# FAVOR+ attention feeding a GEGLU block on one core: attention of the next batch issued beside a token tile, elementwise work in large blocks, output projection as a separate pass

## The chip, the cores and the metric

The kernel runs on one core of a Trainium2 chip. The metric is device time in microseconds (us) of one execution. The engines are TensorE (PE; its weight loads are listed apart as PEld), VectorE (DVE), ScalarE (ACT), GpSimd (POOL) and SyncE (SP). In these kernels matmuls write their results to the memory called PSUM, and most other tiles lie in the one called SBUF. Most executions agree within half a per cent.

Every timed experiment ran beside the kernel before on the same chip. A ratio is the mean time of a kernel's fast runs over that of the kernel before in the same rounds, so it is not quite the quotient of the medians that are quoted beside it.

## The reference

There are 8 batches of 8 heads, 576 positions and 64 dimensions. The attention is linear: positive random features, no softmax matrix. Its output, as 4608 tokens of 512 numbers, goes through a GEGLU block of width 1536.

```python
q_s, k_s = q * scale, k * scale
def phi(x):                                   # 128 features a head
    h = x @ omega.T - sum(x * x) / 2
    return exp(h - max(h)) / sqrt(128)
kv  = phi(k_s).T @ v ;  z = phi(k_s).sum(over positions)
x   = (phi(q_s) @ kv) / (phi(q_s) @ z + 1e-6)  # to (4608, 512)
out = (gelu(x @ w_gate) * (x @ w_val)) @ w_out
```

The maximum is over the features of one position, so the `sum(x*x)` term cancels in it. For q any factor per position cancels in the quotient, so neither kernel takes a maximum for q. For k it must be taken, because the sum over positions weighs positions against each other. Both kernels append a column of ones to v, so that one matmul gives kv and z.

## The kernel before

The attention works head pair by head pair and in pieces of 128 positions. Each step hands a small tile from one engine to the next.

```python
for b in range(B):
    # 15 loads through GpSimd: k, v, q in pieces of 128 positions ...
    for jh in range(NH2):                      # pairs of heads
        for si, (s0, st) in enumerate(s_tiles):   # 5 pieces
            nc.tensor.transpose(kT_ps[:, :st], kslab[:, jh*P:(jh+1)*P], ident[:st, :st])
            nc.vector.tensor_copy(kT_sb[:, :st], kT_ps[:, :st])
            nc.tensor.matmul(proj_ps[:st], kT_sb[:, :st], omega2T)
            nc.vector.reduce_max(nmax[:st], proj_ps[:st]..., negate=True)
            for h2 in range(2):
                nc.scalar.activation(k_p_tiles[si]..., proj_ps..., func=Exp, bias=nmax[:st, h2, :])
        # kz_ps += k_p.T @ v_ext, copied to kz_sb, for the two heads ...
        _try_emit_il(b)        # one gate/value block of token tile 0, from batch 1 on
    for si, (s0, st) in enumerate(s_tiles):
        # transpose q, project, Exp, matmul with kz, divide, transpose x into xT_all ...
        _try_emit_il(b)
```

Only one of the nine token tiles (`N_IL = 1`) gets its gate and value matmuls under the attention. Their results are parked in SBUF and take their Gelu after the last Exp. The other eight tiles follow the attention:

```python
for ti in range(N_IL, N_TOK):
    for jf in range(N_DFF):                    # 12 blocks of 128 columns
        # 4 matmuls g_ps, 4 matmuls vv_ps (512 columns each)
        nc.scalar.activation(g_gelu, g_ps, func=Gelu)
        nc.vector.tensor_mul(gated, g_gelu, vv_ps)
        for q in range(NSUB):                  # output projection, 4 accumulators
            nc.tensor.matmul(out_ps_list[q], gated[:, q*P:(q+1)*P], w_out_sb[:, jf, :], ...)
```

The softmax here doesn't subtract the row's maximum and nothing guards it: scores larger than these inputs give would overflow.

Of the kernel before, what the change touches and what calls it, by code (L numbers as in the profile page):

```python
# [15 lines left out]
def kernel(  # L16
# [11 lines left out]
    nc = tc.nc  # L28
# [3 lines left out]
    assert D == D2  # L32
# [6 lines left out]
    scale = 1.0 / float(D) ** 0.25  # L39

    P = 128
    DFF_TILE = 128
    N_DFF = d_ff // DFF_TILE
    N_DM = d_model // P
    NH2 = H // 2

    singles = ctx.enter_context(tc.tile_pool(name="singles", bufs=1))

    ident = singles.tile([P, P], BF16)
    make_identity(nc, ident)  # L50


    with tc.tile_pool(name="tr_psum0", bufs=1, space=bass.MemoryType.PSUM) as tr_psum0:
        omega_f = singles.tile([M, D], F32)
        nc.sync.dma_start(out=omega_f, in_=omega)
        omega_bf = singles.tile([M, D], BF16)
        nc.scalar.mul(omega_bf, omega_f, scale)
        omegaT_ps0 = tr_psum0.tile([D, M], BF16)
        nc.tensor.transpose(omegaT_ps0, omega_bf, ident)
        omegaT = singles.tile([D, M], BF16)  # L60
        nc.vector.tensor_copy(omegaT, omegaT_ps0)
        omegaT2 = singles.tile([2 * D, M], BF16)
        nc.vector.tensor_copy(omegaT2[:D], omegaT_ps0)
        nc.vector.tensor_copy(omegaT2[D:], omegaT_ps0)
        omega2T = singles.tile([2 * D, 2 * M], BF16)
        nc.vector.memset(omega2T, 0.0)
        nc.vector.tensor_copy(omega2T[:D, :M], omegaT)
        nc.vector.tensor_copy(omega2T[D:, M:], omegaT)
# [3 lines left out]
    w_out_sb = singles.tile([P, N_DFF, d_model], BF16)  # L72

    xT_all = singles.tile([P, N_DM, n_tokens], BF16)

    wg = moe_w_gate.rearrange("(dmo dmi) f -> dmi dmo f", dmi=P)
    wv = moe_w_val.rearrange("(dmo dmi) f -> dmi dmo f", dmi=P)
    wo = moe_w_out.rearrange("(dfo dfi) m -> dfi dfo m", dfi=P)

    def _load_moe_weights():  # L80
        for j in range(N_DM):
            nc.gpsimd.dma_start(out=w_gate_sb[:, j, :], in_=wg[:, j, :])
            nc.gpsimd.dma_start(out=w_val_sb[:, j, :], in_=wv[:, j, :])
        for j in range(N_DFF):
            nc.gpsimd.dma_start(out=w_out_sb[:, j, :], in_=wo[:, j, :])

    DP1 = D + 1

    T_TOK = 512
    N_TOK = n_tokens // T_TOK  # L90
    NSUB = T_TOK // P
    assert n_tokens % T_TOK == 0

    N_IL = 1
    g_all_il = [singles.tile([DFF_TILE, N_DFF, T_TOK], F32, name=f"g_all_il{ti}")
                for ti in range(N_IL)]
    vv_all_il = [singles.tile([DFF_TILE, N_DFF, T_TOK], BF16, name=f"vv_all_il{ti}")
                 for ti in range(N_IL)]
    moe_psum = ctx.enter_context(tc.tile_pool(name="moe_psum", bufs=2, space=bass.MemoryType.PSUM))

    def _moe_gv_jf(ti, jf, ga, va):
        tok = ti * T_TOK
        xT = xT_all[:, :, tok:tok + T_TOK]
        g_ps = moe_psum.tile([DFF_TILE, T_TOK], F32, name="g_ps", tag="gv")
        for jm in range(N_DM):
            nc.tensor.matmul(  # L106
                g_ps, w_gate_sb[:, jm, jf * DFF_TILE:(jf + 1) * DFF_TILE],
                xT[:, jm, :], start=(jm == 0), stop=(jm == N_DM - 1))
        nc.vector.tensor_copy(ga[:, jf, :], g_ps)
        vv_ps = moe_psum.tile([DFF_TILE, T_TOK], F32, name="vv_ps", tag="gv")  # L110
        for jm in range(N_DM):
            nc.tensor.matmul(  # L112
                vv_ps, w_val_sb[:, jm, jf * DFF_TILE:(jf + 1) * DFF_TILE],
                xT[:, jm, :], start=(jm == 0), stop=(jm == N_DM - 1))
        nc.vector.tensor_copy(va[:, jf, :], vv_ps)

    def _il_gen():
        for ti in range(N_IL):
            for jf in range(N_DFF):
                yield ti, jf  # L120
    _il_iter = _il_gen()
    _il_next_b = [1]

    def _try_emit_il(b):
        if b < _il_next_b[0]:
            return
        unit = next(_il_iter, None)
        if unit is None:
            _il_next_b[0] = B + 1
            return  # L130
        ti, jf = unit
        _moe_gv_jf(ti, jf, g_all_il[ti], vv_all_il[ti])
        _il_next_b[0] = ti + 1


    phase1 = ExitStack()
    in_pool = phase1.enter_context(tc.tile_pool(name="in", bufs=2))
    tr_psum = phase1.enter_context(tc.tile_pool(name="tr_psum", bufs=1, space=bass.MemoryType.PSUM))
    work = phase1.enter_context(tc.tile_pool(name="work", bufs=3))
    proj_psum = phase1.enter_context(tc.tile_pool(name="proj_psum", bufs=2, space=bass.MemoryType.PSUM))  # L140
    nd_psum = phase1.enter_context(tc.tile_pool(name="nd_psum", bufs=1, space=bass.MemoryType.PSUM))
    kz_psum_pool = nd_psum
    kz_pool = phase1.enter_context(tc.tile_pool(name="kz", bufs=1))
    xpool = phase1.enter_context(tc.tile_pool(name="x", bufs=2))

    s_tiles = []
    s0 = 0
    while s0 < S:
        st = min(P, S - s0)
        s_tiles.append((s0, st))  # L150
        s0 += st

    k_v = k.rearrange("b h s d -> b s h d")
    q_v = q.rearrange("b h s d -> b s h d")
    v_v = v.rearrange("b h s d -> b s h d")

    NS = len(s_tiles)

    for b in range(B):
        k_in = in_pool.tile([P, NS, H, D], BF16, name="k_in")  # L160
        q_in = in_pool.tile([P, NS, H, D], BF16, name="q_in")
        v_ext = in_pool.tile([P, NS, H, DP1], BF16, name="v_ext")
        nc.vector.memset(v_ext[:, :, :, D:D + 1], 1.0)
        for si, (s0, st) in enumerate(s_tiles):
            nc.gpsimd.dma_start(out=k_in[:st, si], in_=k_v[b, s0:s0 + st, :, :])  # L165
        for si, (s0, st) in enumerate(s_tiles):
            nc.gpsimd.dma_start(out=v_ext[:st, si, :, :D], in_=v_v[b, s0:s0 + st, :, :])  # L167
        for si, (s0, st) in enumerate(s_tiles):
            nc.gpsimd.dma_start(out=q_in[:st, si], in_=q_v[b, s0:s0 + st, :, :])  # L169

        if b == 1:
            _load_moe_weights()

        kz_sb = kz_pool.tile([M, H, DP1], BF16, name="kz_sb")

        for jh in range(NH2):
            h0 = 2 * jh
            k_p_tiles = [work.tile([P, 2 * M], BF16, name=f"k_p{si}", tag=f"k_p{si}")
                         for si in range(NS)]
            for si, (s0, st) in enumerate(s_tiles):  # L180
                kslab = k_in[:st, si, :, :].rearrange("s h d -> s (h d)")
                kT_ps = tr_psum.tile([P, P], BF16, name="kT_ps", tag="trp")
                nc.tensor.transpose(kT_ps[:, :st], kslab[:, jh * P:(jh + 1) * P],  # L183
                                    ident[:st, :st])
                kT_sb = work.tile([P, P], BF16, name="kT_sb")
                nc.vector.tensor_copy(kT_sb[:, :st], kT_ps[:, :st])  # L186

                proj_ps = proj_psum.tile([P, 2 * M], F32, name="proj_ps", tag="prj")
                nc.tensor.matmul(proj_ps[:st], kT_sb[:, :st], omega2T)  # L189

                nmax = work.tile([P, 2, 1], F32, name="nmax")
                nc.vector.reduce_max(nmax[:st],  # L192
                                     proj_ps[:st].rearrange("s (h m) -> s h m", h=2),
                                     axis=mybir.AxisListType.X, negate=True)
                for h2 in range(2):
                    nc.scalar.activation(k_p_tiles[si][:st, h2 * M:(h2 + 1) * M],
                                         proj_ps[:st, h2 * M:(h2 + 1) * M],
                                         func=mybir.ActivationFunctionType.Exp,
                                         bias=nmax[:st, h2, :], scale=1.0)
            for h2 in range(2):  # L200
                h = h0 + h2
                kz_ps = kz_psum_pool.tile([M, DP1], F32, name="kz_ps", tag="nd0")
                for si, (s0, st) in enumerate(s_tiles):
                    nc.tensor.matmul(kz_ps, k_p_tiles[si][:st, h2 * M:(h2 + 1) * M],  # L204
                                     v_ext[:st, si, h, :],
                                     start=(si == 0), stop=(si == NS - 1))
                nc.vector.tensor_copy(kz_sb[:, h, :], kz_ps)  # L207
# [142 lines left out]
```

## Time and profile before

| | |
|---|---|
| time | 574.18 us, median of 3 (573.97 to 574.81) |
| profiled span | 570.9 us |
| first stage: attention, with one tile's gate/value | about 288 us |
| second stage: the other eight tiles | about 283 us |
| one token tile in the second stage | 32.9 us |
| 144 matmuls x 0.216 us, what such a tile streams | 31.1 us |

These rows of the profile page cut the span into 40 equal slices of 14.3 us. A digit is the busy share in tenths. PEclk is the clock that the throttle granted to TensorE.

```profile
PE   3688997767677686767489999999999999999994
DVE  4566876656556565565423242422324242332423
ACT  4563565656656565665822222222222222222220
PEclk9998988756655555565679999999999999999998
```

The two stages are plain to see. From slice 21 on TensorE is full at full clock. Before that no engine stays full, and from slice 7 the clock is at 0.5 to 0.7. The next table has one line per stretch: length, busy time (and instructions) of each engine, granted clock, DMA share, GB/s.

```profile
160.00:180.00 20.00, 15.89 (x124) 9.44 (x123) 12.20 (x45) 11.87 (x30) 12.58 (x15) 0.50 1.24 78
340.00:380.00 40.00, 40.00 (x176) 15.91 (x175) 12.90 (x19) 8.96 (x15) 0.00 (x0) 1.00 0.07 28
```

In the first of these stretches TensorE counts as busy for 79% of the time (72% over the whole first stage), yet the timeline shows mostly the latency of lone matmuls at half clock. The timeline shows one step of the chain (start, length, engine, line, operation, output and inputs, and in brackets how long the engine had waited for whom; weight loads and lines of other steps in between are left out):

```profile
151.98 0.40 PE L189 MATMUL proj_ps<-omega2T,kT_sb 128*128 128x256 bf16 x1 [0.50 <-DVE kT_sb L186]
152.17 0.32 PE L183 MATMUL kT_ps<-ident,k_in 128*128 128x128 bf16 x1
152.41 0.42 DVE L192 TENSOR_REDUCE nmax<-proj_ps 128x2 f32<-128x256 f32 x1 [0.49 <-PE proj_ps L189]
152.75 0.21 DVE L186 COPY kT_sb<-kT_ps 128x128 bf16<-128x128 bf16 x1
152.87 0.62 ACT L196 ACTIVATE k_p_2311<-proj_ps,nmax 128x128 bf16<-128x128 f32 x2 [0.42 <-DVE nmax L192]
153.03 0.40 PE L189 MATMUL proj_ps<-omega2T,kT_sb 128*128 128x256 bf16 x1 [0.49 <-DVE kT_sb L186]
```

One step takes 1.05 us, and PE and DVE each wait half of it for the other. The view of waits (who, for whom, total us, times, longest) has the same pair:

```profile
PEld L189 <- DVE kT_sb L186: 62.2, 110, 1.1
DVE nmax L192 <- PE proj_ps L189: 56.4, 129, 0.9
PE proj_ps L189 <- DVE kT_sb L186: 38.0, 94, 0.9
```

### The profile page before, as it was taken

What the parts mean: (1) busy time and instruction counts of PE and PEld (TensorE: products, weight loads), DVE (VectorE), ACT (ScalarE), POOL (GpSimd) and SP (SyncE); (2) the same over time, 40 slices, a digit from 0 to 9 for tenths busy, and PEclk for the clock granted to TensorE, in tenths of its full rate; (3) what the DMA queues carried; (4) which work ended last, traced back from release to release, by engine and by line L of the source; (5) the groups of instructions that cost most, each with busy time, mean ns of one, the idle gap of its engine ahead of it and who ended that gap; (6) DMA issues with size and microseconds to landing.
All of it is one profiled execution on the core that took longest, in us unless ns stands there. A gap on an engine that the chain in (4) does not pass through costs nothing.

```text
span 570.9 us, 7594 instructions
## 1 busy us (share of the span) xinstructions
PE 480.8 (84%) x2657; PEld 218.3 (38%) x2657; DVE 264.7 (46%) x755; ACT 227.5 (40%) x542; POOL 112.0 (20%) x146
## 2 busy tenths in 40 slices
PE   3688997767677686767489999999999999999994
PEld 1353443424334252433233344334433343333431
DVE  4566876656556565565423242422324242332423
ACT  4563565656656565665822222222222222222220
POOL 9936750806244080000000000000000000000000
PEclk9998988756655555565679999999999999999998
DMA  9999990929859092000001010100101010010101
GB/s 102 143 197 182 112 100 2 112 14 76 51 36 91 0 109 16 1 2 1 1 0 75 0 75 0 56 19 2 73 1 73 0 65 11 15 59 1 73 1 74
DMA packets 120757, 28.83 MB, mean 51 GB/s; under 512 B 113552, under 2 KB 115088, under 8 KB 120720
## 3 DMA queue, kind: packets, MB, share of 16 engines
q0 software_dynamic: 115392, 18.88, 45.2%
q1 hardware_dynamic: 5328, 9.47, 4.3%
q8 instruction: 21, 0.34, 0.3%
q14 instruction: 16, 0.13, 0.1%
HBM read 37.78 MB, written 9.44 MB: 83 GB/s over the span
## 4 chain that ended last, share of the span: by engine, by line
PE 73%; DVE 7%; ACT 6%; issue 5%; POOL 4%; DMA 4%; DVEq 0%; ACTq 0%; POOLq 0%
PE g_ps L296 15%; PE vv_ps L301 14%; PE proj_ps L189 8%; PE kz_ps L204 4%; DVE kT_sb L186 3%; DVE nmax L192 3%; DMA w_val_sb<-in_moe_w_val_dram 3%; PE projqT_ps L226 3%; ACT q_pT L230 2%; PE vv_ps L112 2%; PE g_ps L106 2%; PE xt_ps L251 2%; ACT xT_all L254 2%; POOL v_ext L167 1%; POOL k_in L165 1%
## 5 line engine op out<-in xcount | busy, mean ns | idle before, releaser
L310 DVE TENSOR_TENSOR gated<-g_gelu,vv_ps 128x512 bf16<-128x512 bf16 x96 | 66.0, 688 | 169.2 <-PE vv_ps L301 167.0
L307 ACT ACTIVATE g_gelu<-g_ps 128x512 bf16<-128x512 f32 x96 | 57.3, 597 | 215.1 <-PE g_ps L296 215.1
L296 PE MATMUL g_ps<-xT_all,w_gate_sb 128*128 128x512 bf16 x384 | 100.6, 381 | 0.6 <-ACT g_gelu L307 0.6
L301 PE MATMUL vv_ps<-xT_all,w_val_sb 128*128 128x512 bf16 x384 | 99.6, 379 | 0.0
L192 DVE TENSOR_REDUCE nmax<-proj_ps 128x2 f32<-128x256 f32 (+1 forms) x160 | 67.6, 422 | 60.4 <-PE proj_ps L189 56.4
L189 PE MATMUL proj_ps<-omega2T,kT_sb 128*128 128x256 bf16 (+1 forms) x160 | 59.0, 369 | 39.9 <-DVE kT_sb L186 38.0
L312 PEld LDWEIGHTS <-gated 128*128 128x128 bf16 x384 | 30.2, 97 | 67.7 <-DVE gated L310 44.7
L296 PEld LDWEIGHTS <-w_gate_sb 128*128 128x128 bf16 x384 | 37.5, 98 | 45.9 <-issue 1.0
L301 PEld LDWEIGHTS <-w_val_sb 128*128 128x128 bf16 x384 | 37.5, 98 | 45.3 <-issue 0.3
L165 POOL DMA_DIRECT2D k_in<-in_k_dram x40 | 33.9, 880 | 83.5 <-PE kz_ps L204 79.7
L230 ACT ACTIVATE q_pT<-projqT_ps 128x512 bf16<-128x512 f32 (+1 forms) x80 | 40.6, 552 | 16.1 <-PE projqT_ps L226 14.8
L183 PE MATMUL kT_ps<-ident,k_in 128*128 128x128 bf16 (+1 forms) x160 | 43.2, 270 | 2.5 <-DMA k_in<-in_k_dram 2.5
L189 PEld LDWEIGHTS <-kT_sb 128*128 128x128 bf16 (+1 forms) x160 | 17.1, 107 | 67.5 <-DVE kT_sb L186 62.2
L169 POOL DMA_DIRECT2D q_in<-in_q_dram x40 | 34.0, 913 | 3.7 <-PE qT_ps L216 3.7
L186 DVE COPY kT_sb<-kT_ps 128x128 bf16<-128x128 bf16 (+1 forms) x160 | 32.9, 206 | 2.7 <-PE kT_ps L183 1.9
L167 POOL DMA_DIRECT2D v_ext<-in_v_dram x40 | 34.0, 915 | 0.5 <-issue 0.5
L235 PEld LDWEIGHTS <-q_pT 128*128 128x128 bf16 (+1 forms) x320 | 20.8, 121 | 19.1 <-ACT q_pT L230 16.3
L254 ACT COPY xT_all<-xt_ps 128x512 bf16<-128x512 bf16 (+1 forms) x40 | 21.7, 542 | 15.8 <-PE xt_ps L251 15.1
L251 PE MATMUL xt_ps<-ident,x_sb 128*128 128x128 bf16 (+1 forms) x160 | 18.9, 256 | 7.5 <-ACT xT_all L254 6.6
L183 PEld LDWEIGHTS <-k_in 128*128 128x128 bf16 (+1 forms) x160 | 17.0, 106 | 17.0 <-issue 10.6
L207 DVE CAST kz_sb<-kz_ps 128x65 bf16<-128x65 f32 x64 | 14.3, 223 | 18.4 <-PE kz_ps L204 17.5
L216 PE MATMUL qT_ps<-ident,q_in 128*128 128x128 bf16 (+1 forms) x160 | 21.4, 275 | 0.0
(829 smaller groups left out, 637.5 us busy)
## 6 DMA issues: line engine op xcount, KB each, us to landing
out_dram<-o_sb SPq DMA_DIRECT2D x36, 256.0 KB, 2.0
k_in<-in_k_dram POOLq DMA_DIRECT2D x32, 128.0 KB, 4.2
v_ext<-in_v_dram POOLq DMA_DIRECT2D x32, 128.0 KB, 5.2
q_in<-in_q_dram POOLq DMA_DIRECT2D x32, 128.0 KB, 4.5
w_gate_sb<-in_moe_w_gate_dram POOLq DMA_DIRECT2D x4, 384.0 KB, 11.4
w_val_sb<-in_moe_w_val_dram POOLq DMA_DIRECT2D x4, 384.0 KB, 12.7
w_out_sb<-in_moe_w_out_dram POOLq DMA_DIRECT2D x12, 128.0 KB, 6.7
k_in<-in_k_dram POOLq DMA_DIRECT2D x8, 64.0 KB, 4.3
```

What stands on the lines that cost most here:

```text
L165: nc.gpsimd.dma_start(out=k_in[:st, si], in_=k_v[b, s0:s0 + st, :, :])
L167: nc.gpsimd.dma_start(out=v_ext[:st, si, :, :D], in_=v_v[b, s0:s0 + st, :, :])
L169: nc.gpsimd.dma_start(out=q_in[:st, si], in_=q_v[b, s0:s0 + st, :, :])
L183: nc.tensor.transpose(kT_ps[:, :st], kslab[:, jh * P:(jh + 1) * P], ident[:st, :st])
L186: nc.vector.tensor_copy(kT_sb[:, :st], kT_ps[:, :st])
L189: nc.tensor.matmul(proj_ps[:st], kT_sb[:, :st], omega2T)
L192: nc.vector.reduce_max(nmax[:st], proj_ps[:st].rearrange("s (h m) -> s h m", h=2), axis=mybir.AxisListType.X, negate=True)
L230: nc.scalar.activation(q_pT[:, :, :st], projqT_ps[:, :, :st], func=mybir.ActivationFunctionType.Exp)
L296: nc.tensor.matmul(g_ps, w_gate_sb[:, jm, jf * DFF_TILE:(jf + 1) * DFF_TILE], xT[:, jm, :], start=(jm == 0), stop=(jm == N_DM - 1))
L301: nc.tensor.matmul(vv_ps, w_val_sb[:, jm, jf * DFF_TILE:(jf + 1) * DFF_TILE], xT[:, jm, :], start=(jm == 0), stop=(jm == N_DM - 1))
L307: nc.scalar.activation(g_gelu, g_ps, func=mybir.ActivationFunctionType.Gelu)
L310: nc.vector.tensor_mul(gated, g_gelu, vv_ps)
```

## The change

The attention is rewritten with large instructions, the dense matmuls of a token tile are issued beside the attention of the next batch, and the output projection of a tile comes one iteration later, as a pass of its own. Loads change too: rows are grouped so that four positions of a head are contiguous, and v comes as f32 through SyncE's queue and is converted on GpSimd. ScalarE keeps program order (`manual_schedule`); the order on the other engines is made by the scheduler when the kernel is built. Roughly, issue order is priority, and later work fills gaps.

```diff
+    att = ...tile_pool(name="att", bufs=2, space=PSUM)   # 2 x 2 banks, all attention tiles
+    mo = ...tile_pool(name="mo", bufs=4, space=PSUM)     # 4 x 1 bank, all dense tiles
     ...
-            nc.tensor.transpose(kT_ps[:, :st], kslab[:, jh * P:(jh + 1) * P], ident[:st, :st])
-            nc.vector.tensor_copy(kT_sb[:, :st], kT_ps[:, :st])
-            ...
+        kT = transpose_main(k_in, "k")        # 16 transposes, one copy of 128x2048
+        def k_feat(ps, dst, n):
+            nmax = work.tile([P, n, 1], F32, name="nmax", bufs=4)
+            nc.vector.reduce_max(nmax, ps, axis=AX, negate=True)
+            kd = work.tile([P, n, M], F32, name="kd", bufs=5)
+            nc.vector.tensor_add(kd, ps, nmax.broadcast_to((P, n, M)))
+            nc.scalar.activation(dst, kd, func=Exp)
+        for hp in range(H // 2):
+            pk = att_tile([P, 8, M], F32, "pk")
+            # 4 matmuls of 256 columns
+            k_feat(pk, k_p[:, 2 * hp:2 * hp + 2]..., 8)
+        # the rest of k; then q: transposes, projection, Exps of 128x1024;
+        # then kz; then numerator/denominator, division, transposes into xT of the token tile ...
     ...
+    def gate_val(t):
+        gated = work.tile([P, N_DFF, T_TOK], BF16, name="gated")
+        for jf in range(N_DFF):
+            # 4 matmuls into g_ps (mo)
+            nc.scalar.activation(g_gelu, g_ps, func=Gelu)
+            # 4 matmuls into v_ps (mo)
+            nc.vector.tensor_mul(gated[:, jf, :], g_gelu, v_ps)
+    def project_out(t):
+        for qq in range(NSUB):
+            # 12 matmuls into o_ps (mo), then copy to SBUF and store
     ...
+    with tc.manual_schedule(engines={mybir.EngineType.Activation}):
+        attention(0)
+        for t in range(N_TOK):
+            if t + 2 < B:
+                kq[t + 2] = load_kq(t + 2)
+                vx[t + 2] = load_v(t + 2)
+            if t + 1 < B:
+                attention(t + 1)
+            if t > 0:
+                project_out(t - 1)
+            gate_val(t)
+        project_out(N_TOK - 1)
```

## The prediction

> **What bounds the kernel now.** The profiled span is 570.9 us (timed 574.2) and falls into two stages. From 0 to about 288 us runs the attention with one GEGLU tile's gate/value matmuls interleaved; from 288 us the other eight tiles run alone. In the second stage (timeline, windows) a 512-column matmul starts every 0.216 us at granted clock 1.00, one token tile takes 32.9 us (o_sb of successive tiles: 333.1, 366.0), and 144 x 0.216 = 31.1 us of that is TensorE streaming: it is at its limit. The first stage is a chain of small steps: transpose, kT_sb copy (212 ns), 256-column projection, reduce (424 ns), two Exps (0.31 us each), with about 0.5 us of hand-over at each PE/DVE turn; one step takes about 1.05 us. The waits view shows PE <- kT_sb 38 us, weight loads <- kT_sb 62 us. TensorE is so thin there that the clock falls to 0.50-0.67 from 100 to 300 us. That agrees with the Trainium skill, "TensorE: Matmul & The Clock Gate", Part 1, which says that activity releases the throttle. The attention alone needs little of PE: about 21,000 columns a batch; at full clock the timeline shows transposes 57 ns apart and 65-column matmuls 30 ns apart, so an estimate of 9-10 us a batch.
>
> **What the change does.** It puts eight dense tiles under seven batches of attention.
> - PE floor: 9 x 31.1 + 8 x 10 = 360 us.
> - DVE per batch, scaled from measured durations (256-column reduce 424 ns, 512-column f32 copy 0.68 us, 512-column bf16 PSUM copy 0.42 us): maximum plus subtraction 11 us, transposed copies 3, x and the rest 6.5: 20.5 us; with gated and o_sb 11 us more: 31.5 us.
> - ACT: nine to ten large Exps 9.5 us, twelve Gelus 7.2 us, two table loads at 1.28 us: 19.3 us. The skill ("ScalarE: Activation LUTs", "What ACT_TABLE_LOAD costs") gives 1283 ns for a load; this trace has 1.28.
> So PE stays the limit, at about 40 us an iteration.
>
> **Critical path.** ACT's order is fixed: all Exps of batch b+1, then the Gelus of tile b. The Exp block waits on DVE and a ring of two attention PSUM buffers: I estimate 23 us, in which PE has about 20 us of work (attention 6, output projection 10.4, and gate/value until its four PSUM buffers are full, 3.5). The Gelu block is PE-bound, about 21 us. One iteration: 44 us.
>
> Sum: first batch uncovered, with the input load, 44 us; tile 0 without output projection to fill, 29; six iterations of 44: 264; two tiles without attention 62; last projection 10.4; tail 4: 413, plus 3 us of timing offset and some for an instruction order that fits the real durations badly: **424 us**, range **398 to 460**. Chances: faster by over 2% 0.98, within 2% 0.01, slower 0.01.
>
> **What would show it.** Granted clock near 1.0 after 50 us, mean over 0.93; PE busy over 90% between 75 and 370 us, with short holes in the Exp blocks; tile spacing of 42-48 us, then 31 us for the last two; DVE 270-300 us busy in all; ACT about 170 us with 16-18 table loads; the chain of waits mostly PE, with no k_in or weight DMA after 50 us; the first Gelu at 45-60 us; software-queue packets down to about a third.
>
> **What would make it wrong.** The ring of two PSUM buffers making the Exp block much longer than 23 us (tile spacing over 50, PE waiting on DVE, clock falling); [...]a static instruction order in which PE stalls behind attention while dense work is ready; a first batch longer than 44 us. If the order lets attention's k part run under the Gelu block, iterations near 41 us give about 400.

## The result, and the profile after

The changed kernel takes 422.73 us (median of 4, 422.14 to 424.04); the kernel before took 574.49 in the same rounds. The ratio is 0.7354, 95% interval 0.7335 to 0.7373. The profiled span is 422.2 us. The same four rows (slices of 10.6 us now):

```profile
PE   0456847999999999998999999999999999999995
DVE  1482593649574957495749574957595632433331
ACT  1043046243724362446243624472347221321320
PEclk9999975999999999999999999999999999999999
```

From slice 7 (74 us) TensorE is full at full clock to the end, but for short gaps. What is not full is the start. The parts of the span, as the table of stretches gives them: batch 0 alone; tile 0 with batch 1; six iterations; the last two tiles; the last projection and store.

```profile
0.00:45.40 45.40, 18.82 (x157) 12.55 (x158) 21.04 (x39) 10.40 (x11) 24.54 (x38) 1.00 1.22 211
45.40:92.60 47.20, 37.60 (x252) 20.77 (x256) 27.32 (x42) 17.43 (x23) 10.56 (x14) 0.82 0.76 124
92.60:344.60 252.00, 245.09 (x1782) 127.06 (x1813) 175.89 (x263) 112.47 (x145) 27.78 (x36) 1.00 0.30 59
344.60:406.70 62.10, 61.84 (x284) 28.18 (x288) 22.02 (x32) 14.33 (x24) 0.00 (x0) 1.00 0.12 35
406.70:422.20 15.50, 10.52 (x48) 4.61 (x47) 3.45 (x5) 0.00 (x0) 0.00 (x0) 1.00 0.29 68
```

The six iterations take 42.0 us each on average, with TensorE busy for 97% of them. The table loads of ScalarE mark the two halves of an iteration; here are two full ones (L197 is the load for Exp, L300 the one for Gelu):

```profile
92.64 1.28 ACT L197 ACT_TABLE_LOAD   x1
112.88 1.28 ACT L300 ACT_TABLE_LOAD   x1
134.58 1.28 ACT L197 ACT_TABLE_LOAD   x1
154.83 1.28 ACT L300 ACT_TABLE_LOAD   x1
176.53 1.28 ACT L197 ACT_TABLE_LOAD   x1
```

An Exp block lasts 20.2 us and a Gelu block 21.7. The timeline of TensorE in an Exp block shows how it is filled. Where the chain of before had a wait of half a microsecond, projection matmuls (o_ps) now run (two small groups of transposes are left out):

```profile
176.58 1.06 PE L169 MATMUL kT_ps<-ident,k_in 128*128 128x128 bf16 x16
177.69 1.46 PE L327 MATMUL o_ps<-w_out_sb,gated 128*128 128x512 bf16 x6
178.99 1.04 PE L202 MATMUL pk<-omega2T,kT 128*128 128x256 bf16 x8
179.86 3.40 PE L327 MATMUL o_ps<-w_out_sb,gated 128*128 128x512 bf16 x14
183.17 0.61 PE L202 MATMUL pk<-omega2T,kT 128*128 128x256 bf16 x4
183.62 0.81 PE L327 MATMUL o_ps<-w_out_sb,gated 128*128 128x512 bf16 x3
184.30 0.61 PE L202 MATMUL pk<-omega2T,kT 128*128 128x256 bf16 x4
184.75 3.19 PE L327 MATMUL o_ps<-w_out_sb,gated 128*128 128x512 bf16 x14
```

The pair of waits that ruled the first stage before has its successor in these lines, an eighth of the size:

```profile
PEld L202 <- DVE kd L196: 11.3, 16, 3.2
PE pk L202 <- DVE kd L196: 4.9, 3, 2.7
DVE nmax L194 <- PE pk L202: 4.2, 8, 1.4
```

The start is led by a load. In the chain of work that ended last, these pieces lead from the issue of the loads to the first projection (start, length, what):

```profile
4.99 11.95 DMA q_rest<-in_q_dram
17.44 0.87 PE pk L202 x4
18.33 2.35 DVE nmax L194 x2
```

The transposes of the last 64 positions of q stand before the first projection of k in TensorE's order, and their small load took 12 us to land beside the large ones.

Granted clock: the Trainium skill, "TensorE: Matmul & The Clock Gate", Part 1, says that an activity monitor halves TensorE's clock when it has been idle for a window of about 3.4 us. This trace agrees in direction: 1.00 from 75 us on, where TensorE is dense, 0.52 from 60 to 75 us. But narrow stretches put the drop at 57.5 us, and the longest idle time of TensorE that had ended by then is 1.6 us; in the 3.4 us before the drop it was busy for 1.2 us. So here a window that was mostly idle was enough.

One trap in reading this column: the clock record of the packed trace has its first entry at 50.6 us, and the views show 1.00 where there is no entry. Transposes in that start are some 105 ns apart, against 56 ns in the dense iterations, so TensorE ran at about half rate there, whatever the 1.00 in the first line of the table says.

### The profile page after: what moved, and what is told of

Same layout as the page of the kernel before. It is cut to its first block, busy times and chain, and to the rows that moved or that the text cites. A ratio compares the mean times of both kernels' runs of the same rounds, so it can differ in the third digit from the quotient of the medians.

```text
span 422.2 us, 6222 instructions
## 1 busy us (share of the span) xinstructions
PE 373.9 (89%) x2518; PEld 193.2 (46%) x2561; DVE 249.7 (59%) x380; ACT 154.6 (37%) x202; POOL 62.9 (15%) x87
## 3 DMA queue, kind: packets, MB, share of 16 engines
q0 software_dynamic: 30096, 14.16, 26.6%
## 4 chain that ended last, share of the span: by engine, by line
PE 74%; ACT 9%; DVE 8%; DMA 4%; issue 2%; POOL 1%; SPq 0%; DVEq 0%; POOLq 0%
PE g_ps L297 21%; PE o_ps L327 20%; PE v_ps L303 19%; ACT q_pT L219 6%; DVE nmax L194 3%; DMA q_rest<-in_q_dram 3%; DVE kd L196 3%; PE pk L202 3%; PE nd L250 2%; PE qT_ps L169 2%; PE xt_ps L261 2%; PE kT_ps L169 2%; ACT L300 2%; DMA out_dram<-o_sb 1%; PE kz_ps L235 1%
## 5 line engine op out<-in xcount | busy, mean ns | idle before, releaser
L297 PE MATMUL g_ps<-xT,w_gate_sb 128*128 128x512 bf16 x422 | 115.7, 383 | 4.1 <-ACT g_gelu L300 2.5
L305 DVE TENSOR_TENSOR gated<-g_gelu,v_ps 128x512 bf16<-128x512 bf16 x108 | 73.7, 682 | 72.5 <-PE v_ps L303 65.7
L300 ACT ACTIVATE g_gelu<-g_ps 128x512 bf16<-128x512 f32 x108 | 63.7, 597 | 143.3 <-PE g_ps L297 138.4
L303 PE MATMUL v_ps<-xT,w_val_sb 128*128 128x512 bf16 x414 | 113.0, 382 | 2.4 <-DVE o_sb L330 1.2
L327 PE MATMUL o_ps<-w_out_sb,gated 128*128 128x512 bf16 x417 | 98.2, 379 | 0.7
L197 ACT ACTIVATE k_p<-kd 128x1024 bf16<-128x1024 f32 x32 | 33.8, 1057 | 91.3 <-DVE kd L196 90.1
L303 PEld LDWEIGHTS <-w_val_sb 128*128 128x128 bf16 x432 | 41.1, 99 | 49.1 <-issue 7.0
L297 PEld LDWEIGHTS <-w_gate_sb 128*128 128x128 bf16 x432 | 40.9, 98 | 42.7 <-issue 2.5
L330 DVE COPY o_sb<-o_ps 128x512 f32<-128x512 f32 x36 | 24.0, 683 | 29.2 <-PE o_ps L327 20.7
L194 DVE TENSOR_REDUCE nmax<-pk 128x8 f32<-128x1024 f32 x32 | 37.6, 1217 | 4.2 <-PE pk L202 4.2
L196 DVE TENSOR_TENSOR kd<-pk,nmax 128x1024 f32<-128x1024 f32 x32 | 37.5, 1213 | 0.0
L219 ACT ACTIVATE q_pT<-pq 128x1024 bf16<-128x1024 f32 x32 | 30.2, 1030 | 11.5 <-PE pq L217 11.5
L71 POOL DMA_DIRECT2D k_in<-in_k_dram x8 | 7.2, 906 | 79.5 <-PE rT_ps L182 78.5
```

What stands on the lines that cost most here:

```text
L194: nc.vector.reduce_max(nmax, ps, axis=AX, negate=True)
L196: nc.vector.tensor_add(kd, ps, nmax.broadcast_to((P, n, M)))
L197: nc.scalar.activation(dst, kd, func=Exp)
L219: nc.scalar.activation(q_pT[:, hp].rearrange("m a c p -> m a (c p)"), pq, func=Exp)
L297: nc.tensor.matmul(g_ps, w_gate_sb[:, jm, fs], xT[:, jm, :], start=(jm == 0), stop=(jm == N_DM - 1))
L303: nc.tensor.matmul(v_ps, w_val_sb[:, jm, fs], xT[:, jm, :], start=(jm == 0), stop=(jm == N_DM - 1))
```

## The experiments

All results are correct except that of `x4_no_max`, which is wrong. Times are medians of four fast runs.

### Overlap and block size taken apart

**x1_attention_first** keeps the large blocks but issues all eight batches before the first tile. (Two buffers shrink by one or two, to make room for nine x tiles.)

```diff
-        attention(0)
-        for t in range(N_TOK):
-            ... attention(t + 1); project_out(t - 1); gate_val(t)
+        for b in range(B):
+            attention(b)
+            ...loads of b + 2
+        for t in range(N_TOK):
+            if t > 0:
+                project_out(t - 1)
+            gate_val(t)
```

> All eight attention batches are issued before the first token tile; the large instructions, the loads and the separate output projection stay (buffers shrink a little to make room for nine x tiles). Theory (batching and overlap both pay): attention by itself is paced by VectorE, about 19 us of work a batch plus hand-overs, so some 25 us a batch; 11 us of start + 8 x 25 + 9 x 31.1 + 10 = about 500 us, with a granted clock near 0.5-0.7 in the first 210 us. Rival A (the large blocks are the whole gain, overlap adds little): under 440 us. Rival B (overlap is the whole gain): 550 us or more.

Measured: 550.7 us, ratio 0.957 (0.9542 to 0.9598). My figure of 500 was wrong, and the total lies where rival B put it. The clock row of this run:

```profile
PEclk9999555555555555555799999999999999999999
```

By itself a batch of the rewritten attention takes 32.3 us (the Exps of two successive batches start at 119.05 and 151.37 us). In the kernel before it is 33.2, where no dense matmuls run beside it (xT_all's first copies of batches 1 and 7 start at 73.50 and 272.95 us). The large blocks have fewer hand-overs, but each step is longer, TensorE idles through it at half clock, and the chain is nearly as long as before. Most of the 4% comes from elsewhere: a token tile takes 31.1 us here (its first Gelu and that of the next tile start at 297.31 and 328.39 us) against 32.9 before. Over eight tiles that is 14 of the 21 us by which the span is shorter, and it belongs to the rewritten dense part, not to the attention. Which of its edits does it (the projection as a pass of its own, more PSUM buffers) was not tested. (In this run each batch waits for the one before it to end; an order that overlaps two batches of attention was not tried.)

**x9_before_3_tiles** is the opposite: the kernel before, with its own way of interleaving, for three tiles instead of one.

```diff
-    N_IL = 1
-    g_all_il = [singles.tile([DFF_TILE, N_DFF, T_TOK], F32, ...
+    N_IL = 3
+    g_all_il = [singles.tile([DFF_TILE, N_DFF, T_TOK], BF16, ...
```

> The kernel before, with gate/value of three token tiles under its attention instead of one (its own mechanism, the parked gate values in bf16 so that they fit). This is more overlap without the large blocks. If overlap alone is what pays, each further tile moves some 21 us of dense matmuls into holes of the attention stage, two of them at least 30 us: 530 to 545 us. If the small chained steps leave no usable holes, the attention stage grows by what the second stage loses: 565 us or more.

Measured: 537.77 us, ratio 0.9342 (0.9296 to 0.9388), as the overlap theory said. The parked Gelus of the first tile run at 279.6 us, where they ran at 278.4 before (first line: the kernel before; second: this run):

```profile
278.37 5.32 ACT L281 ACTIVATE g_gelu_il<-g_all_il_86 128x6144 bf16<-128x6144 f32 x1
279.61 5.32 ACT L281 ACTIVATE g_gelu_il<-g_all_il 128x6144 bf16<-128x6144 bf16 x1
```

So the attention stage took two more tiles and grew by 1.2 us. From 73 to 180 us, which holds them, the granted clock is 0.95 instead of 0.65. Two tiles moved under the small steps gain more than all the rewriting did without overlap. How far the kernel before would come with still more tiles was not run.

**x11_small_exps** keeps the changed kernel's overlap and puts back the small Exps for the keys.

```diff
-            kd = work.tile([P, n, M], F32, name="kd", bufs=5)
-            nc.vector.tensor_add(kd, ps, nmax.broadcast_to((P, n, M)))
-            nc.scalar.activation(dst, kd, func=Exp)
+            for i in range(n):
+                nc.scalar.activation(dst[:, i, :], ps[:, i, :], func=Exp,
+                                     bias=nmax[:, i, :], scale=1.0)
```

> As the changed kernel, but the key features take 36 Exps of 128 columns a batch with the maximum as bias, straight from PSUM, as in the kernel before, instead of a subtraction on VectorE and five large Exps. ScalarE gets about 6 us a batch more, VectorE 5.4 us less. Theory (in the overlapped iterations neither engine is the limit, TensorE is): the period of 41.9 us moves by less than 1 us and the total stays within 2% of 422, either side, with a few us won or lost in the first two batches. Rival (the large Exps are what makes the change fast): 440 us or more.

Measured: 427.61 us, ratio 0.7438 (0.7409 to 0.7468): 1.1% more than the changed kernel. The period is 42.7 us (Exp table loads at 90.97, 133.71 and 176.45 us). ScalarE is busy 37 us longer in all, VectorE 37 us less, and hardly any of either shows. Only the keys' Exps are small again here: the large transposes, copies and maxima were not taken apart under overlap.

### What an iteration is bound by

**x4_no_max** takes 79 us of work from VectorE.

```diff
-            (reduce_max, tensor_add)
-            nc.scalar.activation(dst, kd, func=Exp)
+            nc.scalar.activation(dst, ps, func=Exp)
```

> Wrong result on purpose: the maximum and its subtraction are left out of the key features, the Exp reads PSUM itself, so VectorE loses about 10.7 us a batch. Theory (iterations are bound by TensorE, the first 92 us by VectorE): the period of the iterations moves from 41.9 us by less than 1.5 us, the first two batches lose about 10 us each, total 395 to 405 us. Rival (iterations are bound by VectorE's chain): the period falls by 3 us or more and the total below 392.

Measured: 403.82 us, ratio 0.7023. The period becomes 41.1 us (Exp table loads at 77.34, 118.50 and 159.66 us) instead of 41.9. The end of tile 0, marked by the Exp table load after it, comes at 77.3 us instead of 92.6. So of the 20 us that the span lost (402.1 against 422.2), 15 lie in the first two batches (about 20 were expected), and the six iterations give 0.8 each. With TensorE 97% busy this is what a bound by TensorE looks like: removing 10 us of VectorE from a 42 us iteration is worth 2% of it.

**x3_project_same_tile** undoes the lag of the projection.

```diff
-            if t > 0:
-                project_out(t - 1)
             gate_val(t)
-        project_out(N_TOK - 1)
+            project_out(t)
```

> The output projection of tile t is issued right after the gate/value of tile t instead of one iteration later; nothing else changes. Theory: the lag is what gives TensorE 10.4 us of work inside the Exp block; without it the Exp block has only its own 6 us and 3.5 us of gate/value, so each of seven iterations grows by 5 to 10 us: 455 to 490 us, PE busy share in the Exp blocks near one half. Rival: TensorE's order is rebuilt so that attention of the next batch slides under the projection anyway: within 1% of 422.

Measured: 494.37 us, ratio 0.8589 (0.8563 to 0.8615), 17% above the changed kernel and just above the expected range. TensorE's timeline shows why (an extract):

```profile
254.31 10.52 PE L327 MATMUL o_ps<-w_out_sb,gated 128*128 128x512 bf16 x47
264.67 1.06 PE L169 MATMUL kT_ps<-ident,k_in 128*128 128x128 bf16 x16
271.26 0.61 PE L202 MATMUL pk<-omega2T,kT 128*128 128x256 bf16 x4 [0.99 <-DVE kd L196]
275.79 0.60 PE L206 MATMUL pkr<-omega2T,rT 128*128 128x256 bf16 x2 [2.79 <-DVE kd L196]
277.01 1.87 PE L169 MATMUL qT_ps<-ident,q_in 128*128 128x128 bf16 x16 [0.61 <-DVE kd L196]
```

The projection, issued before the next attention, is done in one piece, and then the attention's chain has nothing to be filled with. An Exp block takes 30.9 us here, 10.6 more, where 5 to 10 were expected. It still holds the projection, so the whole 10.4 us has gone from being a filler to being an addition.

**x8_two_banks** takes two of the four PSUM buffers from the dense matmuls.

```diff
-    mo = ...tile_pool(name="mo", bufs=4, space=PSUM)
+    mo = ...tile_pool(name="mo", bufs=2, space=PSUM)
```

> The PSUM buffers of the dense matmuls fall from four to two. Theory (the Exp block is filled by six parts attention, 10.4 us projection and the gate/value blocks that fit into free PSUM buffers): two buffers take 1.7 us of gate/value out of each Exp block, and the Gelu block has less slack, so the period of 41.9 us grows by 2 to 4 us: 435 to 452 us. Rival (the Exp block has work to spare): within 1% of 422.

Measured: 472.17 us, ratio 0.8203 (0.8178 to 0.8229). The direction was right and the size was far off: the period is about 49 us, not 44 to 46. The Gelu block grew from 21.7 to 23.1 us. The Exp block grew from 20.2 to some 26, and for a reason that I had not counted. VectorE's timeline in it (an extract):

```profile
194.54 2.36 DVE L194 TENSOR_REDUCE nmax<-pk 128x8 f32<-128x1024 f32 x2 [0.40 <-PE pk L202]
203.60 0.68 DVE L194 TENSOR_REDUCE nmax<-pkr 128x4 f32<-128x512 f32 x1
204.20 0.68 DVE L330 COPY o_sb<-o_ps 128x512 f32<-128x512 f32 x1
```

The copies that free projection buffers stand behind all key features in VectorE's order, so the first one comes 10 us into the features. Two quarters of the projection fill both buffers by then, and TensorE waits. In the changed kernel the first copy comes as late (189.28 us in a block that starts at 176.5), but four buffers hold four quarters, which is the whole projection. By this trace that is why four are enough and two are not; three buffers, or another order of the copies, were not tried.

**x2_act_order_free** lets the scheduler order ScalarE.

```diff
-    with tc.manual_schedule(engines={mybir.EngineType.Activation}):
+    if True:
```

> ScalarE's order is no longer fixed to program order; everything else as in the changed kernel. Theory: Exps and Gelus mix, table loads rise from 14 to 30 or more at 1.28 us each and some of them fall between a Gelu and the matmuls that wait for its PSUM buffer: 430 to 480 us. Rival: the blocks are not needed because ScalarE is only 37% busy: within 1% of 422.

Measured: 426.86 us (423.85 to 429.13), ratio 0.7415 (0.7369 to 0.746). Table loads rise from 14 to 30, as expected, but the expected 430 to 480 us was wrong: they cost about 1%, with an interval that overlaps the changed kernel's, which is nearly what the rival said. The Trainium skill ("ScalarE: Activation LUTs", "Rules for kernel authors") advises to group functions by table set. The 1.28 us of a load (same page, "What ACT_TABLE_LOAD costs") is confirmed here. The drain of about 1.4 us that the page adds is not seen: in the kernel before, the last Exp and the first Gelu are no further apart than the load (the Exp ends at 286.62 us, the load starts at 286.64, the first Gelu at 287.94). On an engine that is 37 to 41% busy, loads take mostly time that would have been waiting.

### The uncovered start

**x5_start** reorders the first loads.

```diff
+    ident = singles.tile([P, P], BF16); make_identity(nc, ident)   # before the loads
     kq = {0: load_kq(0)}    # k, rest of k, rest of q, q
     vx = {0: load_v(0)}
-        nc.sync.dma_start(out=vf, ...)
+        (nc.gpsimd if b == 0 else nc.sync).dma_start(out=vf, ...)
```

> Only the start changes: the identity is made before the loads are issued, the small rest of q is loaded before the large part of q, and v of batch 0 goes behind q on the same queue instead of beside k on another. In the changed kernel the first projection waited until 17.2 us for the rest of q, which took 12 us to land beside 3 MB of other loads. Theory: k lands at 6 to 7 us, the first projection starts at 8 to 10 us, everything after moves up by 7 to 9 us: 413 to 416 us. Rival: batch 0 is paced by the volume of the loads, so v or q arrive later by as much: within 1% of 422.

Measured: 415.98 us, ratio 0.7232 (0.7205 to 0.7259), as expected. The first transpose starts at 7.4 us instead of 11.2, the first projection at 10.6 instead of 17.2, and tile 0 ends at 84.7 instead of 92.6.

**x6_tile0_under_batch1** gives TensorE more work in the hole between 53 and 69 us.

```diff
+            if t == 0:
+                # after batch 1's key features, before their Exps:
+                attention(1, between=lambda: gate_val(0, 0, 7))
+                gate_val(0, 7)
+                continue
```

> Only tile 0 changes: seven of its twelve gate/value blocks are issued between the key features of batch 1 and their Exps, so ScalarE can give them their Gelus while VectorE makes the features. In the changed kernel TensorE is busy 14.6 of the 23.6 us after 45.4 us because no Gelu may pass before batch 1's Exps, and there is no projection yet to fill. Theory: the hole is a lack of issued work; tile 0 takes 35 to 38 us instead of 47: 410 to 414 us. Rival: the hole is paced by batch 1's own chain and the low clock (0.5 at 60 to 75 us), Exps come later by what the Gelus took, nothing is won: 420 us or more.

Measured: 421.87 us, ratio 0.7341 (0.7303 to 0.7379): nothing won that the rounds can show, so the expected 410 to 414 was wrong. The total is the rival's; its reason is tested in x10. The Gelus were free to go, but the hole stayed:

```profile
50.20 2.36 DVE L194 TENSOR_REDUCE nmax<-pk 128x8 f32<-128x1024 f32 x2 [0.73 <-PE pk L205]
52.47 2.35 DVE L196 TENSOR_TENSOR kd<-pk,nmax 128x1024 f32<-128x1024 f32 x2
59.86 0.68 DVE L313 TENSOR_TENSOR gated<-g_gelu,v_ps 128x512 bf16<-128x512 bf16 x1
```

Here it is again: VectorE makes the features first, the first gated product waits until 59.86 us, and until then v_ps keeps its PSUM buffers, so TensorE stands still from 55.7 to 58.3 us, and dense work stops until 61.

**x7_both** is x5 and x6 together.

> The edits of x5 and x6 together. If both theories hold and the gains are in different stretches they add: 400 to 407 us. If the weights (second and third thirds of gate/value) arrive later than tile 0 asks for them, the gains don't add: 408 us or more.

Measured: 415.46 us, ratio 0.7219 (0.7193 to 0.7246): x5's gain alone. My reason for a failure (late weights) was not the cause: x10 has the same loads and fills the hole.

**x10_fine_tile0** is x7 with another order of issue: two gate/value blocks behind each block of features. This changes VectorE's order, and with it TensorE's and ScalarE's.

```diff
         for hp in range(H // 2):
             ...
             k_feat(pk, ...)
+            if between is not None:
+                between(hp)          # gate_val(0, 2*hp, 2*hp + 2)
```

> As x7, but tile 0's first eight gate/value blocks are issued two at a time behind each block of batch 1's key features. In x6 VectorE ran all features from 50.2 to 59.9 us before the first waiting gated multiplication, so the four PSUM buffers stayed full and TensorE stood still. Theory (VectorE's order, not ScalarE's, kept the hole open): TensorE has no stall over 2 us between 40 and 60 us, tile 0 ends 5 to 10 us earlier than in x7: 404 to 410 us. Rival (the stretch is bound by VectorE's amount of work, the order does not matter): within 1% of 415.

Measured: 409.58 us, ratio 0.7127 (0.7102 to 0.7151). Of the kernels with a correct result it is the fastest, 3.1% below the changed kernel by the quotient of the two ratios. The stretch that had the hole:

```profile
38.00:62.00 24.00, 23.59 (x144) 13.01 (x141) 19.40 (x25) 8.37 (x12) 9.44 (x14) 1.00 1.30 212
62.00:82.00 20.00, 16.98 (x164) 9.91 (x164) 10.38 (x23) 11.09 (x14) 4.57 (x6) 0.91 0.88 162
```

TensorE is busy 98% of the first 24 us, with the same amount of work for VectorE. Tile 0's last Gelu ends at 75.5 us, 9.2 earlier than in x5, and by this mark the next iteration is 4 us longer (45.8 us instead of 41.9). But batch 1's attention is then still running. The transposes of batch 2's keys, with which the next iteration begins on TensorE, start at 79.66 us instead of 84.76, 5.1 us earlier, and the next batch's follow after 41.6 us, as usual. So 5 us were won, and none lost again.

## Why the prediction was right

The time was 422.73 against a predicted 424.0, inside the range of 398 to 460. The total is better than its terms, of which two were off by more than 10 us and partly compensated; that the total came within 2 us is luck:

| term of the sum | predicted | measured |
|---|---|---|
| batch 0 with its loads | 44 | 45.4 |
| tile 0 with batch 1 | 29 | 47.2 |
| six iterations | 264 | 252.0 |
| two tiles without attention | 62 | 62.1 |
| last projection and tail | 14.4 | 15.5 |

The terms sum to 413 us, the span was 422.2. The 8 us that the prediction added for a badly fitting instruction order, and 3 us of offset (1.8 in the profiled run), made up the rest.

- **Bound now.** That the first stage is a chain at half clock, and that the second is at TensorE's limit, held. x9 shows that the chain had room for two more tiles at a cost of 1.2 us.
- **What the change removes.** "PE stays the limit, at about 40 us an iteration" held: 41.9 with TensorE 97% busy, and x4 and x11 show that neither VectorE nor ScalarE sets the period. The estimate of 9 to 10 us of attention a batch is consistent with it (41.9 less 31.1 is 10.8 with the holes).
- **Exp block of 23 us, Gelu block of 21.** Measured 20.2 and 21.7. The 3 us of idle TensorE that were predicted in an Exp block did not come: in the block from 92.64 us it is busy for 20.0 of 20.2 us. That the Exp block is filled by the projection is shown by x3. That two PSUM buffers are too few for it is shown by x8, where I had counted only the gate/value blocks and not the copies that free the projection's buffers.
- **Tile 0 at 29 us is the term that failed**, by 18 us. The prediction took an iteration to get 15 us shorter when there is no projection to fill it. Measured, its two halves are 23.7 us (to the table load at 69.14 us) and 23.5: in the first half TensorE is busy for only 14.6 us, so it waits for batch 1's chain instead of getting done earlier. I had assumed that batch 1's chain would start under batch 0, which the prediction does not say. In the trace its transposes start at 46.9 us, right after batch 0's last matmuls, and the first Gelu comes at 70.4 us, not at 45 to 60. With nothing to project yet, the four PSUM buffers fill by 53.7 us, and TensorE then has only the chain. ScalarE's fixed order holds the Gelus back here. x6 lifts that, and the hole stays open; its trace puts this down to VectorE's order, in which features precede the gated products. x10, with the orders of all three engines changed, closes it.
- **Batch 0 at 44 us was right for a partly wrong reason**: 6 us of it were the wait for the rest of q and the load order, which I had not foreseen (in x5 the first gate matmul starts at 39.2 us instead of 45.4).
- **Smaller signs.** Clock 0.98 (said: over 0.93), but without a record of the first 50.6 us. Tile spacing 41.9 (said: 42 to 48). Software-queue packets 30,096 against 115,392, so a quarter rather than a third. VectorE 249.7 us busy (said: 270 to 300), ScalarE 154.6 with 14 table loads (said: about 170 with 16 to 18): all three were sized too large.

That the blocks of Exp and Gelu matter was not in dispute in the prediction, which took ScalarE's order as given. x2 shows that they are worth about 1%.

What stays open: which edits to the dense part shorten a token tile from 32.9 to 31.1 us, what the large attention blocks other than the keys' Exps are worth under overlap, and how far the small steps of before would come with all tiles interleaved. No run tells these apart.

## What to carry to other kernels

When a chain of small steps and a dense stream share a kernel, put them side by side before making the steps bigger: here the rewriting without overlap was worth 4%, most of it in the dense part, and with overlap the one block size that was tested (the keys' Exps) was worth 1%. Keep some dense work in reserve that depends on nothing recent (here, the projection of the previous tile), issue it after the chain in priority, and give it as many PSUM buffers as it needs until the engine that frees them gets round to it. When TensorE stands still although matmuls are ready, look at the order on the engine that frees their PSUM, not only at the engine that they wait for by name.

## What the Trainium skill lacked or had wrong

- "TensorE: Matmul & The Clock Gate", "Back-to-back issue gap", gives about 131 ns per matmul of 512 columns and about 81 ns for 128 columns as sustained rates in a real kernel with weight loads. These runs show 216 ns (31.1 us for 144 in the last tiles, each matmul with its own weight load) and 56 ns (16 transposes in 1.06 us, less the 0.22 us of the last one). The page's formula for an isolated matmul fits both.
- The same page, Part 4, says that the full clock does not engage for transposes. In the dense iterations transposes start 56 ns apart, at 1.00 granted clock; in the thin start they are some 105 ns apart (16 in 1.89 us, less the last one's 0.31). A transpose inside a dense stream runs at full rate. Whether transposes alone would release the clock, no run here shows.
- The same page, Part 1, ties the halved clock, in its table of the two states, to an idle window of some 3.4 us; further down it has a kernel in which short idle times were enough. The changed kernel is such a case: the clock fell at 57.5 us, when no idle time over 1.6 us had ended and TensorE had been busy for 1.2 of the last 3.4 us.
- The same page, Part 1, warns that recorded clock events can be unreliable. It lacks that the record can begin late: here its first entry is at 50.6 us, and the views read 1.00 before it, while transposes are at the slow spacing just given.
- "ScalarE: Activation LUTs" says to group functions by table set. It lacks that a load is nearly free where ScalarE has slack: 16 more loads of 1.28 us, 20 us of ScalarE, cost about 1% (x2).
- No page says that the order of instructions on VectorE can stall TensorE through PSUM buffers. By the traces it cost 6 us in x7 against x10, and much of the 35 us by which the six Exp blocks of x8 are longer than those of the changed kernel; no run changes VectorE's order alone.
